# Windowed attention and a gated feed-forward on one core: another order of work in the head, and other slots for the attention of batches 1 and 2

## The chip, the core and the metric

The kernel runs on one core of a Trainium2 chip. The core has TensorE (PE, matrix products; its weight loads are a second row, PEld), VectorE (DVE), ScalarE (ACT), GpSimd (POOL), and SyncE (SP), which here only issues DMAs. Each engine works through its own instructions in the order in which the program gives them and waits for others through semaphores. Operands lie in SBUF, the results of TensorE in PSUM, which this program cuts into eight banks of 128 x 512 f32. The metric is the device time of one execution in microseconds (us); the median of five runs is given.

## What is computed

Four batches, eight heads, 768 positions, head dimension 64. Each query sees the last 128 keys and the first four (sinks). Its output, with the heads side by side, goes through a feed-forward: `relu(x Wg) * (x Wv)`, then `Wo`.

```python
def _attn_ref(q, k, v, n_sink, window):
    B, H, S, D = q.shape                      # 4, 8, 768, 64
    scores = np.matmul(q, k.transpose(0, 1, 3, 2)) / np.sqrt(D)
    pos = np.arange(S)
    is_sink = pos[None, :] < int(n_sink)      # 4
    rel = pos[:, None] - pos[None, :]
    keep = is_sink | ((rel >= 0) & (rel < int(window)))   # 128
    scores = np.where(keep, scores, -1000000000.0)
    ...                                       # softmax over the keys
    return np.matmul(a, v)

def _moe_ref(x, w_gate, w_val, w_out):        # x 3072 x 512, d_ff 1536
    return np.maximum(x @ w_gate, 0.0) * (x @ w_val) @ w_out
```

Inputs and output are float32; the kernel multiplies in bfloat16.

## The kernel before

**Units.** Two heads make a pair; a unit is one pair of one batch, sixteen in all (`U[0]` to `U[15]`, four to a batch). For a unit q and k are loaded (`kf`, `qf`: three buffers in turn), cast on GpSimd (`kn`, `qn`: two buffers) and turned so that the head dimension lies on partitions (`KQ`, four buffers; `qT` and `kE` are its parts). Batches 0 and 1 are turned on TensorE (`T_half`, `T`) and copied out of PSUM by ScalarE and VectorE; batches 2 and 3 are turned by DMA: cast, written to DRAM (`td`), read back transposed (`turn`). `kE` holds besides the keys three shifted copies with the sinks ahead, made by `odd_tiles` and `sinks` (lines 181 and 185), on GpSimd except in the half-wise head.

**Attention of a unit.** `Sg(u, s)` multiplies keys and queries of a segment (line 290) into a pair of PSUM banks (`PP[0]` and `PP[1]` by turns, through `pair()`), ScalarE takes the exponential (line 294), and VectorE multiplies by the mask (line 296); in batch 0's segments 0 and 3 TensorE adds the mask first instead (line 286). `W` multiplies by v and divides (lines 321 to 327), and `X` turns the result into `xT` (line 338, copy at line 341); in batches 2 and 3 that goes through DRAM too (`xd`, `xturn`). v is loaded in seven tiles (`load_v`, line 131; tiles 1, 3 and 5 take three DMAs) into one buffer `vf` and cast on GpSimd (line 134).

**Feed-forward.** `chunk(b, g, m)` makes one block of 128 hidden columns for half of a batch's tokens: four gate matmuls (line 356), relu on ScalarE (359), four value matmuls (361), product on VectorE (363). Gate and value banks are taken from `G[0]` to `G[2]` in turn, so the gate matmuls of a chunk need the product (363) of the chunk two before. `ffn2` multiplies by `Wo` (line 388). Weights are loaded by GpSimd (`load_w`, line 190, blocks m0 to m1 of gate and value).

**Order.** All is written out by hand. First a head: batch 0's first halves of the positions (`load_half`, `cast_half`, `T_half` for c = 0 to 3), their attention and the first `X`. Then 96 slots, each one `chunk`, behind which the slot's items of `plan` follow: H is a `T_half` of batch 0's second half, T a `T` of a whole unit, "S12" segment 2 of pair 1, W, X, and F some steps of `ffn2`; from slot 24 on three steps of `ffn2` follow in each slot. Ahead of the chunk stand the slot's items of `prep`: loads, casts, `td`, `turn`, key copies ("sinks"), v loads ("lv") and v casts ("v"). A slot number gives only the place in each engine's order. SP, whose items mostly issue DMAs, and GpSimd run ahead or behind as their waits allow.

DMAs issued by SP and ScalarE use eight semaphores in turn, and each waits until the DMA that had its semaphore before has landed; so eight are on their way at most. `gate(u)` writes two elements of a `kf` buffer so that the load into it can't start before the writing engine has come to that place.

Of the kernel before, what the change touches and what calls it, by code (L numbers as in the profile page):

```python
# [21 lines left out]
def kernel(  # L22
# [112 lines left out]

    def gate(u):

        nc.scalar.copy(kf[u.i % NQ][0:1, 0:2], warm[0:1, :])


    ND = 2 * NP
# [37 lines left out]
    def sinks(u, copy):  # L179
        e = kE[u.i % NT]  # L180
        copy(odd(e)[:, :, 0:4], e[:, 0:4].unsqueeze(1).to_broadcast([128, 3, 4]))  # L181
# [77 lines left out]
        (nc.scalar.copy if u.p < 2 else nc.vector.tensor_copy)(to(qT[t]), vq)  # L259
        odd_tiles(u, nc.gpsimd.tensor_copy)  # L260

    def T_half(c, banks=None):
        t, x = c % NP, c // NP
        tk, tq = banks or (G[3][:, 0:256], G[3][:, 256:512])
        for src, ps in ((kn, tk), (qn, tq)):
            for n in range(3):
                nc.tensor.transpose(ps.bitcast(BF16)[:, 128 * n:128 * n + 128], half(src, c)[:, 128 * n:128 * n + 128],
                                    ident[:])
        vk, vq = (ps.bitcast(BF16)[:, 0:HALF].rearrange("d (n p) -> d p n", p=128) for ps in (tk, tq))
        e = kE[t]  # L270

        for r0, r1, c0 in (((0, 128, 0), (40, 82, ODD + 4), (124, 128, ODD + 140)) if x == 0 else
                           ((0, 128, HALF), (0, 38, ODD + 152), (80, 122, ODD + 276))):
            nc.scalar.copy(e[:, c0:c0 + 3 * (r1 - r0)].rearrange("d (p n) -> d p n", n=3), vk[:, r0:r1])
        (nc.scalar.copy if c == 4 else nc.vector.tensor_copy)(
            qT[t][:, x * HALF:x * HALF + HALF].rearrange("d (p n) -> d p n", n=3), vq)
        if x == 0:
            sinks(U[t], nc.scalar.copy)

    def Sg(u, s):  # L280
        t, bias = u.i % NT, u.b == 0 and s in (0, 3)
        g, b0, n, segs = SEG[s]
        ps = pair()
        if bias:
            for h in range(2):
                nc.tensor.matmul(out=ps[:, h, b0:n], lhsT=ident[:], rhs=mb[:, g, b0:n], start=True, stop=False,
                                 skip_group_check=True)
        for x0, q0, c0, c1 in segs:
            for h in range(2):
                nc.tensor.matmul(out=ps[:, h, c0:c1], lhsT=kE[t][64 * h:64 * h + 64, x0:x0 + 128],  # L290
                                 rhs=qT[t][64 * h:64 * h + 64, q0:q0 + c1 - c0], start=not bias, stop=True,
                                 skip_group_check=True)
        x = ee[u.i % NE][:, g, :, b0:n]
        nc.scalar.activation(x, ps[:, :, b0:n], Act.Exp, bias=0.0, scale=scale)  # L294
        if not bias:
            nc.vector.tensor_tensor(x, x, msk[:, g, b0:n].unsqueeze(1).to_broadcast([128, 2, n - b0]), op=Alu.mult)  # L296

# [97 lines left out]
    with tc.manual_schedule():  # L395
# [3 lines left out]
            load_half(c, (nc.sync, nc.scalar))  # L399
        for j in range(3):  # L400
            load_v(0, j)
        for c in range(4, 6):
            load_half(c)
        setup()
        g = [x[:] for x in G]
        cast_half(0)
        T_half(0, (g[2], g[3]))
        spin(1, 1)
        cast_half(1)
        T_half(1, (g[0], g[1]))  # L410
        Sg(U[0], 0)
        Sg(U[0], 3)
        cast_half(2)
        T_half(2, (g[2], g[3]))
        load_w(0, 2, (0,))
        setup2(1)
        Sg(U[1], 0)
        Sg(U[1], 3)
        cast_half(3)
        T_half(3, (g[0], g[1]))  # L420
        load_w(0, 2, (1,))
        for j in range(3):
            cast_v(0, j)
        load_w(2, 4)
        Sg(U[2], 0)
        Sg(U[2], 3)
        W(U[0], 0, g[2])
        Sg(U[3], 0)
        W(U[1], 0, g[0])
        X(U[0], 0, g[3], nc.vector.tensor_copy)  # L430
        Sg(U[3], 3)
        W(U[2], 0, g[2])
        X(U[1], 0, g[1], nc.vector.tensor_copy)
        W(U[3], 0, g[0])
        X(U[2], 0, g[3])
        X(U[3], 0, g[1])
        cast_half(4)
        cast_half(5)
        load_half(6)
        load_half(7)  # L440
        for j in range(3, 7):
            load_v(0, j)
        load_w(4, 6)
        setup2(2)


# [23 lines left out]
        for b, sl in ((2, {25: "S00 S01", 27: "S02 S10", 29: "S11 S12", 31: "S20 S21", 32: "W0", 33: "S22 S30",  # L470
# [3 lines left out]
            for s, w in sl.items():  # L474
                for y in w.split():
                    put(s, y, b)
# [17 lines left out]
        for b, s0, s1 in ((2, 20, 24), (3, 44, 47)):  # L494
            for j in range(7):
                prep[s0 + j].append(("lv", b, j))
                prep[s1 + j].append(("v", b, j))

        f2 = deque()
        for s, (b, g, m) in enumerate(slots):  # L500
# [38 lines left out]
            for what, i, x in plan[s]:  # L539
                if what == "F":  # L540
                    for _ in range(i):
                        f2.popleft()()
                elif what == "X":
                    X(U[i], x if i < NP else None)
                elif what == "T":
                    T(U[i])
                elif what == "H":
                    T_half(NP + i)
# [47 lines left out]
```

The softmax here doesn't subtract the row's maximum and nothing guards it: scores larger than these inputs give would overflow.

## Time and profile before

| what | value |
|---|---|
| runs, us | 261.75, 256.93, 259.28, 258.45, 257.32 |
| median | 258.45 us |
| profiled execution | 261.75 us, of which span 259.9 us |
| busy, share of the span | PE 241.9 us (93%), PEld 142.0 (55%), DVE 119.2 (46%), ACT 120.5 (46%), POOL 69.5 (27%) |
| mean granted TensorE clock | 0.978 |
| DMA | 40.07 MB, mean 154 GB/s |

Where some slots begin (first gate matmul, us): slot 0 at 17.10, 6 at 32.21, 8 at 40.10, 9 at 41.67, 10 at 43.68, 16 at 56.28, 19 at 64.16, 20 at 68.02, 24 at 78.48, 31 at 94.62, 32 at 101.44, 33 at 106.19, 48 at 139.60, 95 at 239.51.

How to read it: the busy share of TensorE counts matmuls at any clock, so a slow clock looks like work. The page cuts the span into 40 slices of 6.5 us; a digit is tenths of a slice. A group's idle time is that of its engine before it, with what ended it. Durations are those of this one execution.

### The profile page before, as it was taken

Reading aid. Unit: us, or ns where it says so; the run is one execution under the profiler, and the core shown is the slowest. Engines: PE = TensorE matmul, PEld = TensorE weight load, DVE = VectorE, ACT = ScalarE, POOL = GpSimd, SP = SyncE. Lnnn points to the kernel's source line nnn. Section 1 sums busy time; section 2 is a strip of 40 time slices with the busy share of each in tenths; the row PEclk is TensorE's granted clock in tenths of the full one; section 3 lists DMA queues with packets and bytes.
Section 4 is the critical chain, followed back from the end, with each engine's and each line's share of the span. In section 5 each row is a group of like instructions: output and inputs, shape, how many; then the busy total and the mean of one; then the engine's idle time right before and its main releaser. Section 6 shows DMA issues by size and latency. Waiting matters only on the chain.

```text
span 259.9 us, 5295 instructions
## 1 busy us (share of the span) xinstructions
PE 241.9 (93%) x2063; PEld 142.0 (55%) x2084; DVE 119.2 (46%) x219; ACT 120.5 (46%) x222; POOL 69.5 (27%) x126
## 2 busy tenths in 40 slices
PE   7878888997999986999999999999999999999994
PEld 3444565654775543656555555666555555555443
DVE  5454972589963543565323645654232232223000
ACT  3946935888246553443235654542333233333211
POOL 7866726579033226223002610000000000000000
PEclk9999999999799995999999999999999999999999
DMA  6999989989999999689999701244300111100222
GB/s 212 223 255 205 154 236 341 217 199 296 258 249 207 178 209 296 214 246 239 189 206 220 130 24 40 65 108 128 86 30 13 40 40 44 40 32 9 83 113 89
DMA packets 75682, 40.07 MB, mean 154 GB/s; under 512 B 53513, under 2 KB 72713, under 8 KB 75657
## 3 DMA queue, kind: packets, MB, share of 16 engines
q1 hardware_dynamic: 67560, 34.10, 53.5%
q0 software_dynamic: 6864, 4.72, 12.1%
q10 hardware_dynamic: 1232, 0.92, 1.1%
q8 instruction: 16, 0.26, 0.4%
q14 instruction: 10, 0.07, 0.1%
HBM read 28.48 MB, written 11.25 MB: 153 GB/s over the span
## 4 chain that ended last, share of the span: by engine, by line
PE 70%; DMA 17%; issue 4%; ACT 3%; DVE 2%; SPq 2%; POOL 1%; ACTq 0%; POOLq 0%; DVEq 0%
PE g L361 19%; PE g L356 19%; PE g L388 18%; DMA vf<-in_v_dram 7%; PE pp L321 5%; DMA KQ<-kqd 4%; PE pp L388 3%; PE pp L290 3%; DMA kf<-in_k_dram 2%; DMA qf<-in_q_dram 2%; DMA wv<-in_moe_w_val_dram 2%; ACT ee L294 2%; DVE ee L296 1%; SPq L131 1%; SPq L113 1%
## 5 line engine op out<-in xcount | busy, mean ns | idle before, releaser
L363 DVE TENSOR_TENSOR hT<-gs,g 128x384 bf16<-128x384 f32 (+2 forms) x96 | 53.0, 552 | 92.3 <-PE g L361 87.7
L359 ACT ACTIVATE gs<-g 128x384 f32<-128x384 f32 (+2 forms) x96 | 47.7, 497 | 80.0 <-PE g L356 78.0
L356 PE MATMUL g<-xT,wg 128*128 128x384 bf16 (+2 forms) x384 | 79.7, 330 | 2.7 <-DVE hT L363 1.7
L361 PE MATMUL g<-xT,wv 128*128 128x384 bf16 (+2 forms) x384 | 79.4, 330 | 2.6 <-DMA wv<-in_moe_w_val_dram 2.6
L388 PE MATMUL g<-wo,hT 128*128 128x512 bf16 x219 | 61.2, 381 | 1.8 <-issue 0.7
L356 PEld LDWEIGHTS <-wg 128*128 128x128 bf16 x384 | 36.6, 99 | 33.5 <-issue 2.7
L361 PEld LDWEIGHTS <-wv 128*128 128x128 bf16 x384 | 37.7, 99 | 29.6 <-DMA wv<-in_moe_w_val_dram 4.0
L294 ACT ACTIVATE ee<-pp 128x998 bf16<-128x998 f32 (+4 forms) x52 | 44.7, 908 | 13.5 <-PE pp L290 13.2
L296 DVE TENSOR_TENSOR ee<-ee,msk 128x838 bf16<-128x838 bf16 (+3 forms) x44 | 34.6, 797 | 17.8 <-ACT ee L294 17.2
L388 PEld LDWEIGHTS <-hT 128*128 128x128 bf16 x276 | 25.5, 98 | 24.0 <-issue 1.2
L134 POOL CAST vn<-vf 128x512 bf16<-128x512 f32 x28 | 18.6, 685 | 34.3 <-DMA vf<-in_v_dram 34.2
L392 ACT COPY ot<-g 128x512 f32<-128x512 f32 x20 | 11.7, 587 | 20.2 <-PE g L388 19.4
L290 PE MATMUL pp<-KQ 64*128 64x252 bf16 (+6 forms) x328 | 17.4, 225 | 3.8 <-POOL KQ L181 3.5
L321 PEld LDWEIGHTS <-ee 128*128 128x128 bf16 x512 | 19.0, 101 | 2.9 <-issue 0.9
L290 PEld LDWEIGHTS <-KQ 64*128 64x128 bf16 x328 | 11.3, 95 | 14.7 <-issue 9.0
L166 POOL CAST kn<-kf 128x768 bf16<-128x768 f32 x12 | 10.4, 865 | 28.4 <-DMA kqd<-kn 18.4
L321 PE MATMUL pp<-vn,ee 128*128 128x65 bf16 x464 | 17.6, 198 | 0.0
L327 DVE TENSOR_TENSOR xn<-pp,rn 128x896 bf16<-128x896 f32 (+1 forms) x16 | 15.9, 991 | 0.5
L166 POOL CAST qn<-qf 128x768 bf16<-128x768 f32 x12 | 9.9, 828 | 1.8 <-DMA qf<-in_q_dram 1.3
L185 POOL COPY KQ<-KQ 128x372 bf16<-128x372 bf16 x12 | 6.9, 574 | 9.3 <-ACT KQ L258 6.0
L388 PE MATMUL pp<-wo,hT 128*128 128x512 bf16 x36 | 8.1, 379 | 0.0
L341 ACT COPY xT<-g 128x396 bf16<-128x396 bf16 (+2 forms) x8 | 4.5, 562 | 6.8 <-PE g L338 6.8
(74 smaller groups left out, 106.5 us busy)
## 6 DMA issues: line engine op xcount, KB each, us to landing
out_dram<-ot SPq DMA_DIRECT2D x23, 256.0 KB
kf<-in_k_dram SPq DMA_DIRECT2D x12, 384.0 KB
qf<-in_q_dram SPq DMA_DIRECT2D x12, 384.0 KB
vf<-in_v_dram SPq DMA_DIRECT2D x12, 256.0 KB
vf<-in_v_dram SPq DMA_DIRECT2D x12, 224.0 KB
kf<-in_k_dram SPq DMA_DIRECT2D x8, 192.0 KB
wo<-in_moe_w_out_dram POOLq DMA_DIRECT2D x3, 512.0 KB, 14.8
kqd<-qn SPq DMA_DIRECT2D x8, 192.0 KB
```

The costliest lines, as they stand in the source:

```text
L134: copy(vn[b % 2][0:rows, j, :, 0:64], vf[0:rows, j, :, :])
L166: nc.gpsimd.tensor_copy(dst[u.i % 2][:].rearrange("p (n h d) -> p h n d", n=NR, h=2), src[u.i % NQ][:].rearrange("p (h n d) -> p h n d", n ...
L290: nc.tensor.matmul(out=ps[:, h, c0:c1], lhsT=kE[t][64 * h:64 * h + 64, x0:x0 + 128], rhs=qT[t][64 * h:64 * h + 64, q0:q0 + c1 - c0], start ...
L294: nc.scalar.activation(x, ps[:, :, b0:n], Act.Exp, bias=0.0, scale=scale)
L296: nc.vector.tensor_tensor(x, x, msk[:, g, b0:n].unsqueeze(1).to_broadcast([128, 2, n - b0]), op=Alu.mult)
L321: nc.tensor.matmul(out=at[h][:, c:c + 65], lhsT=ee[u.i % NE][:, g, h, c0:c0 + 128], rhs=vn[u.b % 2][:, j, 2 * u.p + h, 0:65], start=c == 0 ...
L327: nc.vector.tensor_tensor(x.rearrange("p t (h d) -> p h t d", h=2), o[:, :, :, 0:64], r.unsqueeze(3).to_broadcast([128, 2, n, 64]), op=Alu ...
L356: nc.tensor.matmul(out=gp[:, 0:n], lhsT=wg[:, ko, m * 128:(m + 1) * 128], rhs=x[:, ko, c], start=ko == 0, stop=ko == KO - 1)
L359: nc.scalar.activation(gs[:, 0:n], gp[:, 0:n], Act.Relu, bias=0.0, scale=1.0)
L361: nc.tensor.matmul(out=vp[:, 0:n], lhsT=wv[:, ko, m * 128:(m + 1) * 128], rhs=x[:, ko, c], start=ko == 0, stop=ko == KO - 1)
L363: nc.vector.tensor_tensor(h[:, m, c], gs[:, 0:n], vp[:, 0:n], op=Alu.mult)
L388: nc.tensor.matmul(out=op, lhsT=hT[b % 2][:, m, t * 128:(t + 1) * 128], rhs=wo[:, m, :], start=m == 0, stop=m == FM - 1)
```

## The change

The head: `load_half` for c = 4 and 5 leaves its place before the one-time set-up, and all of c = 4 to 7 is asked for after the first three v casts and weight blocks 0 to 3 in the program, behind a `memset` on VectorE that writes into `kf[2]`. Weight blocks 0 and 1 are asked for after the fourth cast, both gate and value. The third v tile is cast by VectorE. Segment 0 of pairs 1 and 3 goes into `G[0]` and `G[1]` (two exponentials of one bank each in the place of one over a pair); the other segments name their pairs. The key copies of pair 2 go to VectorE. The `X` copies of the head are all on ScalarE, and both parts of `setup2` come last.

The slots: `gate` writes from VectorE. Batch 1's T, S items move ahead by up to two slots and are spread otherwise; its W and X stay. Batch 2's S and W come three slots later, and its loads, casts, `td`, `turn`, v loads (four slots) and v casts are placed anew.

```diff
     def gate(u):
-        nc.scalar.copy(kf[u.i % NQ][0:1, 0:2], warm[0:1, :])
+        nc.vector.memset(kf[u.i % NQ][0:1, 0:2], 0.0)
...
-    def T_half(c, banks=None):
+    def T_half(c, banks=None, keys=nc.scalar.copy, queries=nc.vector.tensor_copy):
...
-            nc.scalar.copy(e[:, c0:c0 + 3 * (r1 - r0)].rearrange("d (p n) -> d p n", n=3), vk[:, r0:r1])
-        (nc.scalar.copy if c == 4 else nc.vector.tensor_copy)(
-            qT[t][:, x * HALF:x * HALF + HALF].rearrange("d (p n) -> d p n", n=3), vq)
+            keys(e[:, c0:c0 + 3 * (r1 - r0)].rearrange("d (p n) -> d p n", n=3), vk[:, r0:r1])
         if x == 0:
-            sinks(U[t], nc.scalar.copy)
-
-    def Sg(u, s):
+            sinks(U[t], keys)
+        queries(qT[t][:, x * HALF:x * HALF + HALF].rearrange("d (p n) -> d p n", n=3), vq)
+
+    def Sg(u, s, ps=None):
...
-        nc.scalar.activation(x, ps[:, :, b0:n], Act.Exp, bias=0.0, scale=scale)
+        if isinstance(ps, list):
+            for h in range(2):
+                nc.scalar.activation(x[:, h, :], at[h][:, b0:n], Act.Exp, bias=0.0, scale=scale)
+        else:
+            nc.scalar.activation(x, ps[:, :, b0:n], Act.Exp, bias=0.0, scale=scale)
...
-        for c in range(4, 6):
-            load_half(c)
         setup()
         g = [x[:] for x in G]
+        dve = nc.vector.tensor_copy
         cast_half(0)
         T_half(0, (g[2], g[3]))
         spin(1, 1)
         cast_half(1)
         T_half(1, (g[0], g[1]))
-        Sg(U[0], 0)
-        Sg(U[0], 3)
+        Sg(U[0], 0, PP[0])
+        Sg(U[0], 3, PP[1])
         cast_half(2)
-        T_half(2, (g[2], g[3]))
-        load_w(0, 2, (0,))
-        setup2(1)
-        Sg(U[1], 0)
-        Sg(U[1], 3)
+        T_half(2, (g[2], g[3]), dve)
+        Sg(U[1], 0, G[0:2])
+        Sg(U[1], 3, PP[0])
         cast_half(3)
-        T_half(3, (g[0], g[1]))
-        load_w(0, 2, (1,))
+        T_half(3, (g[2], g[3]))
+
+        nc.vector.memset(kf[2][0:1, 0:2], 0.0)
+        load_w(0, 2)
         for j in range(3):
-            cast_v(0, j)
+            cast_v(0, j, copy=dve if j == 2 else nc.gpsimd.tensor_copy)
         load_w(2, 4)
-        Sg(U[2], 0)
-        Sg(U[2], 3)
-        W(U[0], 0, g[2])
-        Sg(U[3], 0)
-        W(U[1], 0, g[0])
-        X(U[0], 0, g[3], nc.vector.tensor_copy)
-        Sg(U[3], 3)
-        W(U[2], 0, g[2])
-        X(U[1], 0, g[1], nc.vector.tensor_copy)
-        W(U[3], 0, g[0])
-        X(U[2], 0, g[3])
-        X(U[3], 0, g[1])
-        cast_half(4)
-        cast_half(5)
-        load_half(6)
-        load_half(7)
+        for c in range(4, 8):
+            load_half(c)
+            if c < 6:
+                cast_half(c)
         for j in range(3, 7):
             load_v(0, j)
         load_w(4, 6)
+        Sg(U[2], 0, PP[1])
+        Sg(U[2], 3, PP[0])
+        W(U[0], 0, g[2])
+        Sg(U[3], 0, G[0:2])
+        W(U[1], 0, g[3])
+        Sg(U[3], 3, PP[0])
+        X(U[0], 0, g[0])
+        W(U[2], 0, PP[1][:, 0, :])
+        X(U[1], 0, g[1])
+        W(U[3], 0, PP[0][:, 0, :])
+        X(U[2], 0, g[2])
+        X(U[3], 0, g[3])
+        setup2(1)
         setup2(2)
...
-        for s, w in {9: "T0", 10: "T1", 11: "T2", 12: "S00 S01", 13: "S02 T3", 14: "S10 S11", 15: "S12", 16: "S20 S21",
-                     17: "S22 S30", 18: "S31 S32", 19: "W0", 20: "W1 X0", 21: "W2 X1", 22: "W3 X2", 23: "X3 F3"}.items():
+        for s, w in {8: "T0", 9: "T1", 10: "S00 S01", 11: "T2", 12: "S02 S10", 13: "T3 S11", 14: "S12 S20", 15: "S21",
+                     16: "S22 S30", 17: "S31 S32", 19: "W0", 20: "W1 X0", 21: "W2 X1", 22: "W3 X2", 23: "X3 F3"}.items():
...
-        for b, sl in ((2, {25: "S00 S01", 27: "S02 S10", 29: "S11 S12", 31: "S20 S21", 32: "W0", 33: "S22 S30",
-                           34: "W1", 35: "S31 S32", 37: "W2", 38: "W3"}),
+        for b, sl in ((2, {28: "S00 S01", 30: "S02 S10", 32: "S11 S12", 34: "S20 S21", 35: "W0", 36: "S22 S30",
+                           37: "W1", 38: "S31 S32", 40: "W2", 41: "W3"}),
...
-        for i, ts in ((8, (13, 17, 18, 20)), (9, (14, 18, 19, 21)), (10, (15, 20, 21, 23)), (11, (19, 21, 22, 25)),
+        for i, ts in ((8, (18, 21, 22, 25)), (9, (19, 22, 23, 26)), (10, (21, 24, 25, 28)), (11, (23, 25, 27, 30)),
                       (12, (28, 31, 33, 36)), (13, (30, 33, 35, 38)), (14, (32, 35, 37, 42)), (15, (34, 37, 39, 43))):
             for t, what in zip(ts, ("rows", "castrows", "td", "turn")):
...
-        for b, s0, s1 in ((2, 20, 24), (3, 44, 47)):
+        for b, s0, s1 in ((2, 24, 28), (3, 44, 47)):
             for j in range(7):
                 prep[s0 + j].append(("lv", b, j))
                 prep[s1 + j].append(("v", b, j))
```

More of the change, by code (lines that the diff above doesn't have):

```diff
@@ L273, in T_half @@
                            ((0, 128, HALF), (0, 38, ODD + 152), (80, 122, ODD + 276))):
-            nc.scalar.copy(e[:, c0:c0 + 3 * (r1 - r0)].rearrange("d (p n) -> d p n", n=3), vk[:, r0:r1])
-        (nc.scalar.copy if c == 4 else nc.vector.tensor_copy)(
-            qT[t][:, x * HALF:x * HALF + HALF].rearrange("d (p n) -> d p n", n=3), vq)
+            keys(e[:, c0:c0 + 3 * (r1 - r0)].rearrange("d (p n) -> d p n", n=3), vk[:, r0:r1])
         if x == 0:
-            sinks(U[t], nc.scalar.copy)
-    def Sg(u, s):
+            sinks(U[t], keys)
+        queries(qT[t][:, x * HALF:x * HALF + HALF].rearrange("d (p n) -> d p n", n=3), vq)
+    def Sg(u, s, ps=None):
         t, bias = u.i % NT, u.b == 0 and s in (0, 3)
         g, b0, n, segs = SEG[s]
-        ps = pair()
+        ps = ps or pair()
+        at = [ps[h][:] if isinstance(ps, list) else ps[:, h, :] for h in range(2)]
         if bias:
             for h in range(2):
-                nc.tensor.matmul(out=ps[:, h, b0:n], lhsT=ident[:], rhs=mb[:, g, b0:n], start=True, stop=False,
+                nc.tensor.matmul(out=at[h][:, b0:n], lhsT=ident[:], rhs=mb[:, g, b0:n], start=True, stop=False,
                                  skip_group_check=True)
@@ L289, in Sg @@
             for h in range(2):
-                nc.tensor.matmul(out=ps[:, h, c0:c1], lhsT=kE[t][64 * h:64 * h + 64, x0:x0 + 128],
+                nc.tensor.matmul(out=at[h][:, c0:c1], lhsT=kE[t][64 * h:64 * h + 64, x0:x0 + 128],
                                  rhs=qT[t][64 * h:64 * h + 64, q0:q0 + c1 - c0], start=not bias, stop=True,
@@ L547 @@
                 elif what == "H":
-                    T_half(NP + i)
+                    T_half(NP + i, queries=nc.scalar.copy if i == 0 else nc.vector.tensor_copy)
                 elif what == "S":
```

## The prediction

> **What bounds the kernel now.** I read the page's busy shares first: TensorE is busy 93% of 259.9 us, so only its pauses can be won or lost. The row of the granted clock then shows two places where TensorE ran slowly, slices 11 and 16 (of 6.5 us each):
>
> ```profile
> PEclk9999999999799995999999999999999999999999
> ```
>
> The 7 and the 5 are stretches at half clock: in the trace's clock records 3.41 us from 64.3 and 6.83 us from 98.4. The timelines of single engines around them say why. At 64.16 TensorE waits for VectorE's gating product (columns: start us, duration us; in brackets the idle time before it and what ended it):
>
> ```profile
> 61.74 0.72 PE L290 MATMUL pp<-KQ 64*128 64x252 bf16 x14
> 64.16 1.30 PE L356 MATMUL g<-xT,wg 128*128 128x372 bf16 x4 [1.71 <-DVE hT L363]
> ```
> ```profile
> 59.13 4.54 DVE L296 TENSOR_TENSOR ee<-ee,msk 128x998 bf16<-128x998 bf16 x2 [0.75 <-ACT ee L294]
> 63.58 0.53 DVE L363 TENSOR_TENSOR hT<-gs,g 128x372 bf16<-128x372 f32 x1
> ```
> ```profile
> 61.53 0.82 POOL L166 CAST kn<-kf 128x768 bf16<-128x768 f32 x1
> 62.30 0.82 POOL L166 CAST qn<-qf 128x768 bf16<-128x768 f32 x1
> 63.07 1.27 POOL L166 CAST kn<-kf 128x768 bf16<-128x768 f32 x1
> ```
>
> Two mask products took 4.54 us (singly 1.43 and 3.19, against a median of 0.68) while GpSimd cast without a pause, and the product that frees the bank stood behind them. The second place:
>
> ```profile
> 98.16 0.61 POOL L134 CAST vn<-vf 128x512 bf16<-128x512 f32 x1 [2.52 <-DMA vf<-in_v_dram]
> 98.72 0.50 POOL L185 COPY KQ<-KQ 128x372 bf16<-128x372 bf16 x1
> 99.16 0.19 POOL L181 COPY KQ<-KQ 128x12 bf16<-128x12 bf16 x1
> ```
> ```profile
> 99.41 0.84 PE L290 MATMUL pp<-KQ 64*128 64x252 bf16 x10 [3.12 <-POOL KQ L181]
> ...
> 101.44 1.49 PE L356 MATMUL g<-xT,wg 128*128 128x384 bf16 x4
> ```
>
> The scores of pair 2, batch 2 (slot 31) wait for key copies that stand in GpSimd's queue behind a cast that waits for v. The four matmuls at 101.44 take 1.28 us from start to start instead of 0.65. Last, the chain that ended last, in order of time, for the start:
>
> ```profile
> 15.72 11.90 DMA vf<-in_v_dram
> 28.38 0.67 POOL wg L190
> 29.05 4.68 DMA wv<-in_moe_w_val_dram
> 33.78 0.80 PE g L361 x4
> ```
>
> Up to 33.8 us transfers decide: the fourth v tile lands at 27.6, its cast holds GpSimd's queue, and weight blocks 6 and 7 are asked for behind it. After slot 48 (139.6 us) TensorE has no pause over 0.3 us.
>
> The sums are against the profiled execution: 261.75 us, the span and 1.85 around it. It was the slowest of five (median 258.45). I deduct nothing for that: the two pauses are the likeliest thing to be smaller in the other runs, so a kernel without them needs no second deduction.
>
> **Head: +0.4.** Scores in the G banks free the pairs sooner, and with the key copies of pair 2 moved to VectorE (0.48 + 0.30 + 0.21 + 0.24 us of ScalarE at 8.53) they shorten chains that end in the first gate matmul at 17.1. That is cover only: the value matmul then waits until 18.77 for wv. What counts is the order of transfers. SP's first second-half load goes from 8.09 to behind the memset on kf[2], which follows VectorE's last query copy: 10.9, for in before that copy ends at 11.0. The loads behind it on SP (eight halves, v tiles 3 to 6) wait too. Low end 0.3: the queue was still moving v until 11.6, so its next bytes went out at about 11.6; from 10.9 plus 1.0 (issue to first packet at 32.91) it is 11.9. High end 2.8: all of SP's delay. GpSimd asks for wg 0-1 at 9.2 instead of 8.14, wv at 9.95 as before, blocks 2-3 at 11.9 instead of 12.35, so the weights give back little. I take 0.4, near the low end, since bytes and not issues fill this stretch. Moving the one-time masks behind the head costs nothing: they are needed at 22.4. All X copies on ScalarE: 0.47 each, beside idle ScalarE.
>
> **The gates for the loads of units 4 to 6, ScalarE to VectorE: 0.** ScalarE passed them at 32.7; VectorE gets there after its last mask, 33.9, and 0.4 later still for the head. Unit 4's cast moves from 36.27 to about 37.9; its transposes come at 42. Cover 2.5 us. Everything else on SP behind them (unit 7, batch 1's v) moves by as much; the v casts have about 1 us left.
>
> **Batch 1 a slot sooner: +1.2.** T0 goes into slot 8, and GpSimd's key copies for it now stand ahead of unit 5's casts, which T1 in slot 9 needs. The trace has the same sequence one slot later:
>
> ```profile
> 44.41 0.50 POOL L185 COPY KQ<-KQ 128x372 bf16<-128x372 bf16 x1 [1.84 <-ACT KQ L258]
> 44.84 0.20 POOL L181 COPY KQ<-KQ 128x12 bf16<-128x12 bf16 x1
> 44.98 0.83 POOL L166 CAST kn<-kf 128x768 bf16<-128x768 f32 x1
> 45.75 0.84 POOL L166 CAST qn<-qf 128x768 bf16<-128x768 f32 x1
> ```
>
> Its T began at 43.01, so keys are cast 2.8 us and queries 3.6 us after T0's start. TensorE is there after 0.67 (T0) + 1.34 (chunk 9) = 2.01: it waits 0.79, transposes 0.34, waits 0.44: 1.23 in all. The request for weight blocks 8 to 11 sits behind these casts: 45.7 instead of 41.09. With the old flights (8.7 and 11.5 us) wv lands at 57.9; slot 16 needs it at about 58.4. Bounds 0 and 2.0; I take 0. Later slots: ScalarE's work from slot 10 to 17 sums to 15.0 us against TensorE's 15.4; the relu of slot 18 behind two exponentials costs 0.2.
>
> **The pause at 64.16: -3.35, of which +1.0 returns.** It cost 1.71 idle, and slot 19 took 3.86 instead of 2.22 at half clock: 3.35. Here a rule speaks otherwise. The Trainium skill, "TensorE: Matmul & The Clock Gate", section "Why this matters for your kernels", puts a throughput drop behind idle gaps over about 3 us; by it this gap is worth 1.71 alone. The trace has the half clock right behind a 1.71 us gap, so 3.35. In the new plan slot 18 has no scores, but the product of slot 17 still stands behind two masks (S22, S30) with only 0.4 us of slack, and v casts run at that time. The skill's "SBUF — State Buffer", section "Who interferes with whom", says that a VectorE instruction with two SBUF inputs and a GpSimd instruction that reads SBUF exclude each other for one whole instruction. By that a mask loses at most one cast, 0.6 us, so the stall is 0.2. The row above lost 2.5 us to four casts in a row: stall 2.1, and with the slow clock all 3.35. I take 1.0, between them, because the casts of units 8 and 9 will hardly have landed when the v casts end.
>
> **Batch 2 three slots later: -5.8.** The pause at 96.3 cost 3.1 idle and 2.7 of half clock (2.03 instead of 1.2 to slot 32, 4.75 instead of 2.92 in it). SP and GpSimd run by order, not by slot, so I follow their queues. rows 8 to 10 go out as before behind batch 1's v, row loads 11 as before. But v tile 0 now precedes turn 8, td 10 and v tile 1 precede turn 9, and rows 12 precede v tile 4. With the old durations (turn 2 to 5 us each) turn 10 starts at 87 and lands at 92; rows 12 land at 95.3; GpSimd casts them and v tiles 3 and 4 and has pair 2's key copies by 98.1. TensorE, 3 slots later and some 1.5 us ahead, asks at 99.6: no wait, 1.5 us to spare. xturn 11, now in slot 44, lands 9 to 10 us after slot 42 begins; slot 48 comes 11.7 after it. Bounds 0 and 5.8 kept.
>
> **Sum:** 261.75 + 0.4 + 1.2 + 0.2 - 3.35 + 1.0 - 5.8 = **255.4**; the bounds of the single terms give it 253.0 to 257.5.
>
> **Rivals.** (1) *Masks starved again*: GpSimd's v casts meet S22 and S30 and the whole 3.35 returns: 255.4 + 2.35 = 257.8. For it: the 3.19 us row, the 0.4 us of slack. Against: at 55 us casts and masks met and the masks took 0.68 and 0.79. (2) *Slower: GpSimd's queue again, now behind rows 12.* The casts of unit 12 stand ahead of pair 2's key copies; each microsecond that they land after 96.8 stops TensorE in slot 34, and from 1.7 of idle 2.7 of slow clock join. At 3.5 us that is 255.4 + 6.2 = 261.6, over the median of before; it is slower by 1% from 3.0 us on. For it: SP's transposes last up to 5.22 us. Against: 1.5 us of margin. (3) *The head does not do what it says*: all 2.8 us of SP's delay reach the weights: 257.8. For it: the chain above runs through these very loads. Against: the queue was full.
>
> **How the numbers follow.** Forecast 0.48, rival 1 0.20, rival 2 0.19, rival 3 0.13. A measurement of this kernel can tell about 1%, 2.6 us: faster means under 255.9. Of the forecast's case four in five lie there (0.38), and 0.04 of rivals 1 and 3: faster 0.42. Slower (over 261.0) is rival 2 from 3.0 us on and mixtures of rivals 1 and 3: 0.20. The rest, 0.38, is within 1%. The range goes to 252.8 (no stall returns, the weights no later) and to 261.6 (rival 2).
>
> **What would show it.** Right: no idle over 1.7 us on TensorE after slot 8, no 5 in the clock row; about 0.8 and 0.4 us of wait for GpSimd at T1; weight blocks 6 and 7 landing 0.3 to 0.8 later than 33.7. Wrong: slot 34's or 36's scores waiting for L181; the value matmul of slot 16 waiting for wv; slot 19 waiting for L363 by over 1.7; slot 48 waiting for xT.

## Result: no change that can be measured, and the profile after

Median 257.78 us over 27 runs, against 257.87 us of the kernel before over 48: ratio 0.9991, interval 0.997 to 1.0013. (Ratios and their intervals leave out executions over 1.5% longer than the kernel's fastest; medians are of all executions.) The forecast, 255.4, was 2.4 us too low. The profiled execution of the changed kernel took 257.17 us (span 255.2), 4.6 us less than the profiled one of before; but that one, the slowest of the 48 runs, was no usual one.

The clock row has no digit under 9 any more, where before it had a 7 and a 5:

```profile
PEclk9999999999999999999999999999999999999999
```

The timeline of TensorE in the places that the prediction named (start, duration, instruction; in brackets the idle time before it and its releaser). In the listing of the changed kernel, and of every kernel with its head, the lines behind 290 stand four further down: gate matmul L360 (before 356), value L365 (361), gating product L367 (363), `W` L325 (321), mask product L300 (296). L254 are the transposes of a `T`, L259 is the copy of its queries.

```profile
43.09 0.83 PE L365 MATMUL g<-xT,wv 128*128 128x396 bf16 x4
44.61 0.51 PE L254 MATMUL g<-ident,kn 128*128 128x128 bf16 x6 [0.69 <-POOL kn L166]
...
51.18 0.37 PE L290 MATMUL pp<-KQ 64*128 64x252 bf16 x8
52.12 0.39 PE L290 MATMUL pp<-KQ 64*128 64x244 bf16 x6 [0.56 <-DVE KQ L259]
...
64.95 0.79 PE L360 MATMUL g<-xT,wg 128*128 128x372 bf16 x4 [0.93 <-DVE hT L367]
...
103.37 0.53 PE L325 MATMUL pp<-vn,ee 128*128 128x65 bf16 x12
105.37 0.22 PE L325 MATMUL pp<-vn,ee 128*128 128x65 bf16 x2 [1.47 <-POOL vn L134]
105.93 0.70 PE L325 MATMUL pp<-vn,ee 128*128 128x65 bf16 x18 [0.34 <-POOL vn L134]
```

The first wait is the foreseen one at T1 (0.69 us, then 0.26 for the queries), the third the part of slot 19's pause that the prediction let return. The second and the last were not foreseen. In slot 12 the last six score matmuls belong to pair 1; they need the pair of PSUM banks in which T2 has left pair 2's turned queries, and VectorE's copy out of it (L259) comes late. VectorE in slot 12 and ahead of slot 19:

```profile
50.64 0.55 DVE L367 TENSOR_TENSOR hT<-gs,g 128x396 bf16<-128x396 f32 x1
51.12 0.94 DVE L259 COPY KQ<-pp 128x768 bf16<-128x768 bf16 x1
...
61.37 3.08 DVE L300 TENSOR_TENSOR ee<-ee,msk 128x838 bf16<-128x838 bf16 x2 [0.35 <-ACT ee L298]
64.37 0.53 DVE L367 TENSOR_TENSOR hT<-gs,g 128x372 bf16<-128x372 f32 x1
```

The product at 50.64 stands behind two mask products that took 2.08 us from 48.65, while GpSimd cast without a pause from 47.31 to 51.40; those ahead of slot 19's product took 3.08 us. The median of a single one is 0.69.

In slot 35 `W` of unit 8 waits 1.81 us for v. The old wait of slot 31 for key copies (3.12 us before) is gone. GpSimd's timeline shows what stands ahead of the last two v casts:

```profile
102.27 0.83 POOL L166 CAST kn<-kf 128x768 bf16<-128x768 f32 x1 [1.80 <-DMA kf<-in_k_dram]
103.43 0.88 POOL L166 CAST qn<-qf 128x768 bf16<-128x768 f32 x1 [0.33 <-DMA qf<-in_q_dram]
104.26 1.62 POOL L134 CAST vn<-vf 128x512 bf16<-128x512 f32 x2
```

These are the casts of unit 13, batch 3, which wait for rows that have only just landed. The chain that ended last goes the same way (start, duration, what):

```profile
98.34 0.22 SPq L175
98.56 0.04 issue
98.60 0.58 SPq L161
99.18 0.04 issue
99.23 4.08 DMA qf<-in_q_dram
...
104.26 1.63 POOL vn L134 x2
105.89 0.04 issue
105.93 0.70 PE pp L325 x18
```

From 90 us up to 98.34 the chain is mostly TensorE's own work. From there SP's queue decides: a transpose (L175), behind it unit 13's rows (L161, 4.08 us until the queries land), behind them the casts, v, and TensorE.

### The profile page after: what moved, and what is told of

Same layout as the page of the kernel before. It is cut to its first block, busy times and chain, and to the rows that moved or that the text cites. A ratio compares the mean times of both kernels' runs of the same rounds, so it can differ in the third digit from the quotient of the medians.

```text
span 255.2 us, 5302 instructions
## 1 busy us (share of the span) xinstructions
PE 238.2 (93%) x2063; PEld 139.7 (55%) x2084; DVE 119.9 (47%) x226; ACT 120.0 (47%) x219; POOL 71.4 (28%) x125
## 4 chain that ended last, share of the span: by engine, by line
PE 72%; DMA 11%; issue 5%; ACT 4%; POOL 3%; SPq 3%; DVE 2%; ACTq 0%; POOLq 0%; DVEq 0%
PE g L360 20%; PE g L365 19%; PE g L392 18%; DMA qf<-in_q_dram 8%; PE pp L325 5%; PE pp L392 3%; PE pp L290 3%; ACT ee L298 2%; DMA wv<-in_moe_w_val_dram 2%; SPq L113 1%; DMA vf<-in_v_dram 1%; SPq L131 1%; ACT ot L396 1%; POOL vn L134 1%; PE g L342 1%
## 5 line engine op out<-in xcount | busy, mean ns | idle before, releaser
L367 DVE TENSOR_TENSOR hT<-gs,g 128x384 bf16<-128x384 f32 (+2 forms) x96 | 52.9, 552 | 89.8 <-PE g L365 84.5
L365 PE MATMUL g<-xT,wv 128*128 128x384 bf16 (+2 forms) x384 | 78.1, 326 | 3.3 <-DMA wv<-in_moe_w_val_dram 2.5
L360 PE MATMUL g<-xT,wg 128*128 128x384 bf16 (+2 forms) x384 | 78.5, 326 | 1.3 <-DVE hT L367 0.9
L392 PE MATMUL g<-wo,hT 128*128 128x512 bf16 x219 | 60.4, 379 | 1.9 <-issue 0.6
L360 PEld LDWEIGHTS <-wg 128*128 128x128 bf16 x384 | 36.1, 98 | 32.0 <-issue 1.1
L365 PEld LDWEIGHTS <-wv 128*128 128x128 bf16 x384 | 37.3, 98 | 29.4 <-DMA wv<-in_moe_w_val_dram 4.4
L298 ACT ACTIVATE ee<-pp 128x838 bf16<-128x838 f32 (+4 forms) x50 | 43.0, 904 | 11.4 <-PE pp L290 11.3
L300 DVE TENSOR_TENSOR ee<-ee,msk 128x838 bf16<-128x838 bf16 (+3 forms) x44 | 34.8, 799 | 14.7 <-ACT ee L298 14.0
L134 POOL CAST vn<-vf 128x512 bf16<-128x512 f32 x27 | 19.2, 736 | 23.3 <-DMA vf<-in_v_dram 23.3
L325 PEld LDWEIGHTS <-ee 128*128 128x128 bf16 x512 | 17.9, 97 | 4.6 <-issue 2.5
L325 PE MATMUL pp<-vn,ee 128*128 128x65 bf16 x488 | 17.8, 193 | 1.8 <-POOL vn L134 1.8
L331 DVE TENSOR_TENSOR xn<-pp,rn 128x896 bf16<-128x896 f32 (+2 forms) x18 | 17.0, 943 | 0.6
L290 PE MATMUL pp<-KQ 64*128 64x3 bf16 (+5 forms) x316 | 15.8, 221 | 0.6 <-DVE KQ L259 0.6
L166 POOL CAST qn<-qf 128x768 bf16<-128x768 f32 x12 | 10.9, 906 | 2.5 <-DMA qf<-in_q_dram 2.2
L345 ACT COPY xT<-g 128x372 bf16<-128x372 bf16 (+2 forms) x10 | 5.4, 545 | 5.6 <-PE g L342 5.6
```

Source lines behind the costliest of these rows:

```text
L134: copy(vn[b % 2][0:rows, j, :, 0:64], vf[0:rows, j, :, :])
L166: nc.gpsimd.tensor_copy(dst[u.i % 2][:].rearrange("p (n h d) -> p h n d", n=NR, h=2), src[u.i % NQ][:].rearrange("p (h n d) -> p h n d", n ...
L290: nc.tensor.matmul(out=at[h][:, c0:c1], lhsT=kE[t][64 * h:64 * h + 64, x0:x0 + 128], rhs=qT[t][64 * h:64 * h + 64, q0:q0 + c1 - c0], start ...
L325: nc.tensor.matmul(out=at[h][:, c:c + 65], lhsT=ee[u.i % NE][:, g, h, c0:c0 + 128], rhs=vn[u.b % 2][:, j, 2 * u.p + h, 0:65], start=c == 0 ...
L331: nc.vector.tensor_tensor(x.rearrange("p t (h d) -> p h t d", h=2), o[:, :, :, 0:64], r.unsqueeze(3).to_broadcast([128, 2, n, 64]), op=Alu ...
L360: nc.tensor.matmul(out=gp[:, 0:n], lhsT=wg[:, ko, m * 128:(m + 1) * 128], rhs=x[:, ko, c], start=ko == 0, stop=ko == KO - 1)
```

## The experiments

Ratios are to the kernel before, run on the same chip in the same session; intervals are 95%. "Unit 4's load" is the start of SP's first row load behind the gates, the first thing that the head can delay on SP.

### The parts alone

`before_again` is the kernel before once more, unchanged. `head_only` takes the change's hunks down to `setup2(2)`, with the gates; the other two take one hunk of the slots each:

```diff
 # batch1_only
-        for s, w in {9: "T0", 10: "T1", 11: "T2", 12: "S00 S01", ...
+        for s, w in {8: "T0", 9: "T1", 10: "S00 S01", 11: "T2", ...
 # batch2_only
-        for b, sl in ((2, {25: "S00 S01", 27: "S02 S10", ...
+        for b, sl in ((2, {28: "S00 S01", 30: "S02 S10", ...
-        for i, ts in ((8, (13, 17, 18, 20)), ...
+        for i, ts in ((8, (18, 21, 22, 25)), ...
-        for b, s0, s1 in ((2, 20, 24), (3, 44, 47)):
+        for b, s0, s1 in ((2, 24, 28), (3, 44, 47)):
```

> The kernel before, unchanged, profiled a second time. Theory A (the profiled execution of before was not a usual one: most of its 9 us in two pauses with half clock are absent elsewhere): span 254.5 to 256.5 us, mean clock 0.99 or more, the scores of slot 31 wait under 1.5 us for the key copies of line 181, and the wait for line 363 near slot 19 is under 1.2 us. Theory B (the pauses are there each time, and the change gives the gain back elsewhere): span 258 or more, clock 0.985 or less, over 2.5 us of wait at slot 31.

Measured: 258.85 us in its profiled execution, 257.61 the median of 36 runs of before in that session. The same two pauses are there, smaller and with less slow clock. TensorE's timeline:

```profile
63.59 0.79 PE L356 MATMUL g<-xT,wg 128*128 128x372 bf16 x4 [1.68 <-DVE hT L363]
...
97.55 0.84 PE L290 MATMUL pp<-KQ 64*128 64x252 bf16 x10 [2.40 <-POOL KQ L181]
98.33 1.46 PE L388 MATMUL g<-wo,hT 128*128 128x512 bf16 x3
```

After the first the gate matmuls run at full speed (0.79 for four, before 1.30); after the second the clock is halved for 3.41 us and not for 6.83. The two profiled executions of before are 2.90 us apart, and all of it lies in these places (slot 48 begins 3.08 us sooner). Neither theory came true as written: the waits are there each time, 4.08 us together against 4.83, and what was out of the ordinary is mainly the slow clock, 3.41 us of it against 10.24.

> The kernel before with the head of the change alone (and the gates on VectorE); all slots as before. Prediction's term: +0.4 us (ratio 1.0015). Rival 3: +2.8 us (1.011). If the earlier weight order helps: down to -0.8 us (0.997).

Measured: ratio 1.006 (1.0033 to 1.0088), +1.5 us. Slot 8 begins 0.86 us later than in `before_again`, slot 25 only 0.13 (slot 19 waits 0.95 us there, 0.73 less than in `before_again`), slot 32 again 1.11. So this pair of profiles has the loss in batch 2's old plan, where scores wait for turned keys in slots 25 to 31, 3.9 us in all (`before_again`: 3.1):

```profile
81.27 0.28 PE L290 MATMUL pp<-KQ 64*128 64x244 bf16 x2 [0.78 <-DMA KQ<-kqd]
81.97 0.53 PE L290 MATMUL pp<-KQ 64*128 64x252 bf16 x10 [0.42 <-POOL KQ L181]
...
87.78 0.28 PE L290 MATMUL pp<-KQ 64*128 64x252 bf16 x4 [0.85 <-POOL KQ L181]
...
98.71 0.80 PE L290 MATMUL pp<-KQ 64*128 64x252 bf16 x10 [1.88 <-POOL KQ L181]
```

Unit 4's load stands at 33.80 us, against 32.89 in `before_again`, and the turns of units 8 to 11 go out 1.3 to 2.3 us later. The head's price is paid 50 us later, through SP.

> The kernel before with batch 1's slots of the change alone. The wait of T1 for GpSimd's casts, 1.2 us, and 0.5 us for the copy of pair 2's queries show in the profile under either theory. Theory A: little is saved at slot 19 in a usual execution, so +1 to +2 us (ratio 1.004 to 1.008). Theory B: the pause at slot 19 shrinks by 2.35 us, so -1 us or less (0.996).

Measured: 1.0008 (0.9981 to 1.0035). T1's wait is there (0.68), the wait for the query copy too (0.56), and slot 19 waits 2.45 us. The time lies between the two theories; the pause at slot 19 did not shrink, as theory B needed.

> The kernel before with batch 2's slots, loads, casts and turns of the change alone. Theory A: the usual wait at slot 31 is small, and the new wait of W for v in slot 35 (1.5 to 1.8 us in the trace of after) takes its place: -1 to +1.5 us (ratio 0.996 to 1.006). Theory B: 5.8 us less 1.8 us, so -4 us (0.985).

Measured: 0.992 (0.9889 to 0.9951), and 0.986 (0.9818 to 0.9903) when it was run again as `batch2_again`: 2.0 and 3.6 us under before, more than any other part and between the two theories, the second nearer to B. In the profile of `batch2_only` TensorE has no pause over 0.4 us after 69 us, and `W` of slot 35 runs through:

```profile
103.08 1.13 PE L321 MATMUL pp<-vn,ee 128*128 128x65 bf16 x32
```

> The same kernel as batch2_only once more (before with batch 2's plan alone), so that the next ones can be compared with it on one chip: ratio 0.992 to before again, some 2 us. If it is 0.997 or more, its first interval was lucky and the sum of the parts has to be taken anew.

In this second profile TensorE is 1.5 us sooner at slot 35 (100.26 us for 101.78), and there `W` waits 0.79 us for v even in this kernel; slot 48 then waits for x:

```profile
134.00 0.32 PE L356 MATMUL g<-xT,wg 128*128 128x384 bf16 x1 [1.05 <-DMA xT<-xd]
```

So the batch 2 part alone brings about as much as the whole change was forecast to bring; it is taken back when the others join. SP's own timelines show where the queue runs late. `batch2_only`, then the changed kernel:

```profile
86.75 2.33 SPq L175 DMA_TRANSPOSE KQ<-kqd  x1
89.12 0.59 SPq L161 DMA_DIRECT2D kf<-in_k_dram  x1
...
96.73 0.40 SPq L131 DMA_DIRECT2D vf<-in_v_dram  x1
```
```profile
90.42 2.00 SPq L175 DMA_TRANSPOSE KQ<-kqd  x1
92.47 0.58 SPq L161 DMA_DIRECT2D kf<-in_k_dram  x1
...
99.74 0.40 SPq L131 DMA_DIRECT2D vf<-in_v_dram  x1
```

These are unit 10's turn, the load of unit 12's keys and the last v tile of batch 2. TensorE reaches slot 35 at 101.78 and 102.07, almost together; SP is 3.0 us later at the last v tile.

### The parts left out, and the gate

```diff
 # no_head: before, with batch 1's and batch 2's hunks
 # no_batch1: the changed kernel, with batch 1's line of before
 # scalar_gate: the changed kernel with
-        nc.vector.memset(kf[u.i % NQ][0:1, 0:2], 0.0)
+        nc.scalar.copy(kf[u.i % NQ][0:1, 0:2], warm[0:1, :])
```

> The kernel after with the head and the gates of before (so both slot parts alone). Theory A (the parts' costs add up: head +1.5, batch 1 +0.2, batch 2 -2.0 us): median 255.9 (ratio 0.993), unit 4's loads from about 33 us, batch 2's first row load at 55.8 instead of 57.28, W's wait in slot 35 0.5 us or less. Rival B (batch 1's plan alone delays SP enough: in it the row load of unit 11 went out at 68.4 us, against 65.8 before): W still waits 1.2 to 1.8 us, median 257.3.

> The kernel after with batch 1's slots of before (head with gates, and batch 2). Theory A (the parts add up): 257.6 + 1.5 - 2.0 = 257.1 (ratio 0.998), no waits at T1, but W in slot 35 still waits for v, 1 to 2 us. Rival B (the head's +1.5 us arose in batch 2's old plan, where scores waited for turned keys; three slots later that is hidden): no wait in slot 35, median 256.0 (ratio 0.994); then head and batch 1 together make the wait of the kernel after.

Measured: `no_head` 0.9968 (0.9936 to 1.0), `no_batch1` 0.9991 (0.9965 to 1.0017), so each of the two other parts takes back a good half of what batch 2 gives, or all of it, and both together no more than the head alone; the interval of `no_head` still overlaps that of `batch2_only`. In both profiles `W` waits for v in slot 35: 1.20 us in `no_head`, 1.97 in `no_batch1`. That speaks for rival B of the first, though its profiled execution, 261.7 us, had half clock twice and 2.45 us of wait at slot 19 ahead of that place; and for theory A of the second, whose TensorE has no pause over 1 us between slot 2 and slot 35:

```profile
104.19 0.22 PE L325 MATMUL pp<-vn,ee 128*128 128x65 bf16 x2 [1.63 <-POOL vn L134]
104.74 0.70 PE L325 MATMUL pp<-vn,ee 128*128 128x65 bf16 x18 [0.34 <-POOL vn L134]
```

> The kernel after, with the gates of units 4 to 6 written from ScalarE as before. Theory A (SP's queue is delayed at the gates and carries the delay to batch 2): VectorE wrote the gates at 34.58 us, ScalarE is past its last exponential of that place at 34.0; the loads of unit 4 start 0.6 us sooner (34.1 for 34.73), the first row load of batch 2 about 0.6 sooner, v tile 6 of batch 2 0.6 sooner, W's wait in slot 35 falls from 1.8 to about 1.2, median 257.2 (ratio 0.998). Rival (the gates cost nothing, as the prediction had it): loads sooner but W's wait and the time as they were, 257.8.

Measured: 1.0008 (0.9981 to 1.0035), so no gain. Unit 4's load starts 1.58 us after slot 6 instead of 2.18, the 0.6 us expected, and `W` waits 1.31 us instead of 1.81; but slot 48 now waits 0.59 us. The step at the gate is seen in the trace, not in the time; the smaller wait of `W` can't be put down to it, since TensorE itself came to slot 35 1.4 us later here (103.45 for 102.07).

### The waits taken away

`v_first` puts the casts of units 12 to 15 behind batch 2's v casts in GpSimd's order, and their `td` and `turn` behind these. `v_late` also puts the turns of units 14 and 15 behind batch 2's x transposes on SP. `t1_early` puts unit 5's casts a slot sooner. All three start from the changed kernel; `both2` is the last two together, and `head_v_late` is `v_late` with batch 1's old line.

```diff
                       (12, (28, 31, 33, 36)), (13, (30, 33, 35, 38)), (14, (32, 35, 37, 42)), (15, (34, 37, 39, 43))
 # v_first
+                      (12, (28, 35, 36, 39)), (13, (30, 36, 37, 41)), (14, (32, 38, 39, 43)), (15, (37, 40, 41, 44))
 # v_late, both2, head_v_late, best
+                      (12, (28, 35, 36, 39)), (13, (30, 36, 37, 41)), (14, (32, 38, 39, 45)), (15, (37, 40, 41, 47))
 # t1_early, both2
-        prep[8] += [("kq", 4), ("load", 7), ("lv", 1)]
-        prep[9] += [("kq", 5), ("w", 8, 12)]
+        prep[8] += [("kq", 4), ("kq", 5), ("load", 7), ("lv", 1)]
+        prep[9] += [("w", 8, 12)]
```

> The kernel after, with the casts of units 12 to 15 put three slots later in GpSimd's order (and their td and turn behind them), so that batch 2's v casts stand ahead of them. Theory A (the W of slot 35 waits 1.8 us because v tiles 5 and 6 stand behind GpSimd's cast of unit 13's rows, and nothing is late next): slot 35's W starts without a wait over 0.4 us, the end comes about 1.5 us sooner, median 256.3 (ratio 0.994). Rival B (SP's whole queue is about 3 us late in the kernel after, the last v tile itself lands at 103.5 us, and so v is late with or without the casts): the wait shrinks to no less than 1 us, median 257.3. Rival C (batch 3's turns, now later, make slot 48 wait): a new wait at slot 48 or 50, median 258 or more.

Measured: 0.998 (0.9945 to 1.0015), 0.3 us better than the changed kernel's own ratio where 1.5 were expected. `W` no longer waits, but slot 48 does, and SP's timeline shows a turn (L175) between the last two x transposes (L155):

```profile
129.59 1.85 SPq L155 DMA_TRANSPOSE xT<-xd  x1
131.49 1.48 SPq L175 DMA_TRANSPOSE KQ<-kqd  x1
133.07 1.22 SPq L155 DMA_TRANSPOSE xT<-xd  x1
```
```profile
136.23 0.32 PE L360 MATMUL g<-xT,wg 128*128 128x384 bf16 x1 [0.85 <-DMA xT<-xd]
```

This is rival C, in part: one wait had covered the next. In the changed kernel the same transpose landed at 134.76 us; the matmul that reads it, slot 48's fourth, comes at 135.4 (slot 48 begins at 134.93, each matmul takes 0.16), so the cover was 0.6 us. In this profile slot 19 waited 1.69 us besides, against 0.93 in that of the changed kernel.

> The kernel after once more, on one chip with the next three. Expected: within 0.3% of before (ratio 0.997 to 1.003), and W's wait for batch 2's v in slot 35 between 1 and 2 us again, since SP's queue is some 3 us later than in batch2_only. If the wait is gone here, the 1.8 us of the first profile were chance.

> The kernel after with the casts of units 12 to 15 behind batch 2's v casts and the turns of units 14 and 15 behind batch 2's x transposes (so both2 without the earlier casts of unit 5). Theory A (the place behind SP's queue, W's wait and slot 48's together, holds back 1.8 us): no wait over 0.5 us in slots 35 to 48, 1.5 to 1.8 us under after_again. Rival B (the wait at T1 is the larger part): under 0.8 us.

> The kernel after with unit 5's casts a slot sooner. Theory A (what TensorE wins at T1 it waits away in slot 35, because v comes by SP's queue, which does not get earlier): the 0.7 us wait and the 1.3 us at T1 go, W's wait grows by about as much, to 2.5 to 3 us, and the time stays within 0.5 us of after_again. Rival B (the waits add): 1.2 us under after_again.

> no_batch1 (head, gates and batch 2's plan) with the same later casts and turns as v_late. Theory A (the new head costs its time only through SP's queue, by W's wait of 1.97 us in no_batch1): no wait over 0.5 us in slots 35 to 48, 1.8 us under no_batch1's ratio of 0.999, so 0.992 or less. Rival B (the head costs 1 us or more of TensorE's own waits before slot 8): 0.996 or more.

Measured on one chip: `after_again` 0.9993 (0.9964 to 1.0022), with 1.97 us of wait in slot 35, so that wait is no chance. `v_late` 0.9976 (0.9941 to 1.0011): its profile has no wait over 0.3 us from slot 20 to slot 95, but it is only 0.9 us under `after_again` by the medians, 0.4 by the ratios, and the intervals overlap; slot 19 waited 1.69 us. `t1_early` 0.9988 (0.9958 to 1.0017): no gain, as theory A said, but not by theory A's way. T1 doesn't wait and `W` doesn't either; TensorE lost the time in between, at the query copy, ahead of which two mask products took 3.36 us, and in slot 19:

```profile
52.25 0.39 PE L290 MATMUL pp<-KQ 64*128 64x244 bf16 x6 [1.71 <-DVE KQ L259]
...
68.56 0.79 PE L360 MATMUL g<-xT,wg 128*128 128x372 bf16 x4 [2.75 <-DVE hT L367]
```

`head_v_late` 0.9957 (0.9928 to 0.9987), and no wait from slot 35 to 48. Against `no_batch1`'s 0.9991 that is 0.9 us of 1.97: between theory A and rival B, so part of the head's cost does not run through `W`'s wait, if the difference holds: the intervals overlap. Which part was not settled.

> The kernel after with three things undone that it was seen to wait for: unit 5's casts moved ahead (the casts a slot sooner, against the 0.7 us wait at T1), the casts of units 12 to 15 behind batch 2's v casts (against W's 1.8 us), and the turns of units 14 and 15 behind batch 2's x transposes (against v_first's 0.85 us at slot 48). Theory A (these waits are what kept the kernel after from its forecast): no wait over 0.4 us at T1, slot 35 or 48, median 2 to 2.5 us under after, 255.4 (ratio 0.990). Rival B (another pause takes the gain, as in v_first where the median moved 0.3 us): 257 or more; then the waits seen in one profile are not what sets the median.

> both2 once more (v_late and t1_early together). v_late alone gave 0.9976, t1_early alone 0.9988. Theory A (the two places are one behind the other, so each edit alone only uncovers the other's wait, and together they free more than their sum): 0.993 or less, some 1.8 us or more under before. Rival B (both2's first 0.989 was lucky and the edits merely add): 0.9955 to 0.998.

Measured: 0.9892 (0.9842 to 0.9942), then 0.9921 (0.9897 to 0.9944). Both intervals lie under the changed kernel's 0.9964 to 1.0022. Against its ratio of 0.9993 the two edits alone moved 0.17% and 0.05%, together 0.7 and 1.0%: theory A's figures, not rival B's. The medians, 255.59 and 256.05 us, are 1.9 and 2.3 us under before in the same sessions, where the forecast was 2.5 us under (255.4 for 257.87): these waits together are most of what kept the kernel from there. How one hands on to the other is argued, not shown: the profile of `both2_again` still waits 1.71 us for the query copy and 0.93 in slot 19, and the intervals of the single edits are wide enough that their sum could reach the same.

### Towards a better version

```diff
 # spread: batch2_only with
-   17: "S22 S30", 18: "S31 S32", 19: "W0",
+   17: "S22", 18: "S30 S31", 19: "S32 W0",
 # best: spread with the line of v_late
```

> batch2_only with the mask products of batch 1 spread by a slot: S22 alone in slot 17, S30 and S31 in 18, S32 in 19. Theory A (slot 19's gate matmul waits, 1.7 us in batch2_only, because the product of slot 17 stands behind two masks slowed by GpSimd's casts): the wait falls under 0.5 us, median 1.2 us under batch2_only. Rival (the masks meet the casts wherever they stand, the wait only moves to slot 20 or to W1): a wait of 1 us or more in slots 19 to 21, no gain.

> spread with the casts, td and turns of units 12 to 15 later: the casts behind batch 2's v casts, the turns of units 14 and 15 behind the x transposes of batch 2 on SP. In v_first W's wait went, but slot 48 then waited 0.85 us for the x transpose of unit 11, which stood behind the turns of units 14 and 15. Theory A (with those turns behind it slot 48 has its x): no wait over 0.4 us from slot 35 to slot 48, and from slot 48 to 95 99.9 us; median as spread or up to 1 us under it, 253.5 to 254.5 against 257.8 of before. Rival: batch 3's scores (slot 54, 57) then wait for their turned keys, and it comes out slower than spread.

> best once more, on the same chip as both2: ratio 0.985 to 0.990 as before. Theory A (the old head and the old plan of batch 1 are worth keeping): 0.5 us or more under both2. Rival B (they are worth nothing once the casts and turns stand late): equal to both2 within 0.4 us.

Measured: `spread` 0.9871 (0.9822 to 0.9921) beside `batch2_again`'s 0.986: no gain. In its profile slot 19 doesn't wait, as theory A said, but TensorE, ahead by that, waits 2.19 us for v in slot 35. `best` 0.9847 (0.9798 to 0.9897) and 0.9872 (0.9837 to 0.9906), medians 254.42 and 254.18 us against 257.48 and 258.34 of before: it is 1.3 to 1.5% under before, 0.9% at the least by the intervals (six executions each time). The changed kernel was not run beside it; its own ratios, 0.9991 and 0.9993, lie as far above. In its first profile slot 19 still waits 2.27 us, so spreading the masks is no cure, and nothing waits over 0.3 us after that; in the second an `X` of slot 20 waits 1.74 us and `W` of slot 35 0.49. In the session that they share it is 1.9 us under `both2_again`; the intervals of the ratios overlap a little.

## Why the prediction was wrong, step by step

**The base: right.** "I deduct nothing" rested on the two pauses being the part of the profiled run that was out of the ordinary. They were: the 2.90 us between the two profiled executions of before lie in them, by their slow clock more than by their idle time.

**Head +0.4, gates 0: right where they were looked at, wrong behind it.** Slot 6 begins 0.3 us later than before, and the value matmul that waits for weight blocks 6 and 7 starts 0.1 later (33.86). Over all twenty profiles slot 8 begins at 39.9 us with the old head and at 40.6 with the new (medians of 9 and 11, which range over 3 us). But unit 4's load went from 32.91 to 34.73 us, of which the gate is 0.6 by `scalar_gate` (medians: 32.9 with the old head, 34.9 with the new head and its gates on VectorE). The prediction saw that what stands behind the gates "moves by as much" and asked only whether batch 1's v casts had cover. The delay goes on through SP: the row loads of batch 2 start at 57.28 us and those of unit 11 at 70.84, in `batch2_only`, which has the same plan for batch 2, at 54.59 and 66.32.

**Batch 1 +1.2: right, and incomplete.** At T1 TensorE waited 0.69 and 0.26 us where 0.79 and 0.44 were worked out. The 0.56 us for the copy of pair 2's queries out of the PSUM banks was not in the sum: the prediction added up ScalarE's work from slot 10 to 17 and left out VectorE's, where masks slowed beside GpSimd's casts stood ahead of the copy.

**The pause at 64.16, -3.35 + 1.0: right in this execution, too small in most.** 0.93 us idle came back, without slow clock. But in six of the ten profiles with this plan of batch 1 slot 19 waits 1.68 to 2.75 us, and with the old plan 1.68 to 1.72 in four of seven. So the new plan took nothing off the usual pause; only the slow clock of that one execution of before was gone. The rule of one cast for a mask, from which the prediction had 0.2, did not hold either: the two masks took 3.08 us, and one alone 3.19 in the profile of before.

**Batch 2 -5.8: the step that failed.** It took "row loads 11 as before" and followed the queues, with "the old durations"; that gave turn 10 from 87 to 92 us and rows 12 at 95.3. `batch2_only`, whose SP isn't delayed, had turn 10 from 86.75 to 91.19 and rows 12 landed at 93.11 and 94.33: the working is good for that kernel. In the changed one turn 10 went out at 90.42 and rows 12 landed at 95.85 and 96.96, since SP's delay, which the prediction itself had named at the head and the gates, was not carried into this step. And the queue was followed to pair 2's key copies only. These came in time, so rival 2 as it was written didn't happen; one place further the casts of unit 13 stood ahead of v, with the very mechanism of rival 2. Unit 13's rows landed at 102.12 and 103.30 us, the last v tile at 103.49 (in `batch2_only` at 99.07, 100.06 and 100.25), and TensorE stood 1.81 us at a place up to which the prediction had not followed the queue. `t1_early` shows the same floor from the other side: TensorE reached slot 35 at 105.56 us, 3.5 later than in the changed kernel, did not wait there, and began slot 36 only 1.4 later.

The sum with what was missed, 255.4 + 1.8 (`W` for v) + 0.6 (query copy) = 257.8, meets the measured median, but partly by chance: it takes the waits of one execution, leaves out the larger pause at slot 19 of most others, and `v_late`, without `W`'s wait, won 0.4 to 0.9 us and not 1.8. How the loss divides between these waits stays open; that together they make most of it is what `both2` shows. Part by part, in ratios: head +0.6%, batch 1 +0.1%, batch 2 -0.8 and -1.4%; together -0.1%.

**The rivals.** Rival 1, which put the time at 257.8 as well, is not ruled out by the profiled execution: masks were slowed there too, those of slots 10 and 16, and in most other executions its wait at slot 19 came, mostly without the slow clock. Rivals 2 and 3 did not come as written: slot 34 did not wait for L181, and the weights were not 2.8 us late. The signs of being right came true or nearly so (the weights came 0.1 us later, not 0.3 to 0.8), and nothing was won: none of them stood at slot 35, and `W`'s wait there came in two pieces, 1.47 and 0.34 us, each under the 1.7 that was looked for. The range from 253.0 to 257.5 does not follow from the bounds of the single terms: the upper ones of the head (2.8), of the weights for slot 16 (2.0) and of the pause (3.35) alone lead to 262.2.

**The rule on the clock.** The prediction weighed the Trainium skill's page "TensorE: Matmul & The Clock Gate" (section "Why this matters for your kernels": a drop behind idle gaps over about 3 us) against the 1.71 us gap with half clock behind it, and took the trace as certain. The other profiles say: neither. In all twenty traces TensorE has 29 idle times of 1.6 to 3.12 us between 15 and 245 us; behind 12 of them (a window that begins between 0.5 us before the idle time and 1.8 after it), by the clock records, the clock is halved for 3.41 us or 6.83. A thirteenth such stretch begins 1.84 us after `W`'s wait in `after_again`; the only other one, in `no_head`, follows waits of 0.98 and 1.12 us in slot 6. The length does not decide: behind 1.67 us (slot 6 of `head_v_late`) the clock was halved, behind 2.75 us (slot 19 of `t1_early`) it stayed whole. By these counts a pause of this size is worth its idle time, and in under half of the cases some 1.7 us more (an estimate: half of 3.41).

## What to carry to other kernels

A delay found in one step of a prediction has to be put into every later step that uses the same queue: here SP was 1.8 us late at its gates and 3 us late at the transfers that a gain 60 us further on rested on. Follow a moved queue until its last consumer, not until the wait that the change removes; an operand that arrives by a queue sets a floor, and TensorE's time saved ahead of it turns into a wait there. When one wait is taken away and little is won, look for the next one behind it (here `W`, then slot 48). And look at more than one execution: the pause at slot 19 was 0.93 us in the profile of the changed kernel and 1.68 or more in six of the nine others with its plan of batch 1.

## What the runs showed of the hardware

The granted clock falls in whole windows: the clock records of all twenty profiles have half clock 14 times, for 3.41 us or twice that, and in no other length but where the span ends. The same pause, in the same place and of the same length to 0.05 us, has such a window behind it in one execution and none in another (1.71 us in slot 19 of before, 1.68 in `before_again`; 1.71 us at the query copy in `t1_early` with it and in `both2_again` without). What decides between the two is open.
